# Modulation gates read back through DRAM, eight LayerNorm-1 tiles transposed by DMA in groups of four, loads in halves, and another order of tasks

## The chip, the cores and the metric

One NeuronCore of one Trainium2 chip runs the whole computation as one program. The metric is the time of the program on the device in microseconds (us). Before the change it is 209.67 us, the median of three runs (209.31 to 209.95).

A core has five instruction queues: TensorE (PE: matmuls, with PEld for the weight loads), VectorE (DVE), ScalarE (ACT), GpSimd (POOL) and SyncE (SP), which here issues nearly all DMAs. Each engine works off its queue in order and waits on semaphores of the others.

## The reference

One transformer block for 2048 tokens of width 512, with a linear attention of 32 heads and a gated feed-forward part of width 1376. A vector c gives six modulation vectors of 512: shift, scale and gate for each of the two parts.

```python
mod = (_silu(c) @ w_mod).reshape(c.shape[0], 6, 1, -1)
sa, ca, ga, sb, cb, gb = (mod[:, 0].copy(), mod[:, 1].copy(), mod[:, 2].copy(), mod[:, 3].copy(), mod[:, 4].copy(), mod[:, 5].copy())
h = _layernorm(x, axis=-1) * (1 + ca) + sa
x = x + ga * _A_ref(h, A_wqkv, A_w_phi, A_wo)
h = _layernorm(x, axis=-1) * (1 + cb) + sb
x = x + gb * _B_ref(h, B_w_gate, B_w_up, B_w_down)
```

In `_A_ref` q and k go through a small matrix per head, then through softmax(p) and softmax(-p) over the 16 features of a head; keys times values are summed over all tokens (kv), and each query's row is multiplied with that sum and divided by its normaliser. `_B_ref` is (sigmoid(h @ w_gate) * (h @ w_up)) @ w_down.

## The kernel before, in words

The 2048 tokens are 16 tiles of 128. All work is written as named tasks in a graph (`Graph`, line 103). A task has a name, one engine or a choice of engines, the keys that it reads and writes, and its buffers. The text `ORDER` (lines 35 to 81) lists every task once; `arrange` (line 131) walks it, takes the engine after an @ (A is ACT, D is DVE, P is POOL) or the first that the task allows, hands out buffers from fixed sets in the order in which they come free, and each engine gets its tasks in that order. The costs written beside the tasks do nothing when the kernel runs.

The names, in the order of the data:

- **ld_...** (lines 655 to 678): loads, issued by SP. x in pieces (x0a, x0b, x1, x2, x3), the thirds of wqkv (wk, wv, wq), w_mod (wm00 and wm01: shift and scale of the first part, one half of the rows each; wmga: its gate; wmm2: all three vectors of the second part), and wo, wg, wu, wd.
- **warm0, warm1_i** (line 711): matmuls on zeros ahead of the real work. **c1, c2, c3**: silu(c).
- **modc1, modc2** (line 717): shift and scale as columns, one column of 128 values per one-column matmul, 32 matmuls each; **modc1c, modc2c** copy them out of PSUM. **scb, ga, gb** (lines 693 and 898 to 906): silu(c) spread over 128 columns and multiplied with the gate's part of w_mod by four 512-column matmuls, so that the gate stands in every partition; **gac, gbc** copy it to SBUF. **wo0..3** and **wd0..10** multiply the rows of wo and wd with it (lines 908 and 917).
- **tpw, wTc, fold, foldc, wqT** (line 735): the small matrix w_phi is folded into the weights of q and k; wqT are DMA transposes.
- First LayerNorm (lines 775 to 840), in the groups of `LG`: **st1** statistics, **rs1** the inverse root, **nmr1** minus mean times it, **xn1** the normalised tile. Where `TD` is 0 the tile is transposed on TensorE (**tph**) and **hm1** applies scale and shift out of PSUM; where `TD` is 1 SP issues a DMA transpose per tile (**xT1**, line 816) and hm1 works in place in SBUF. hm1_20 is column block 0 of group 2.
- **K, V, Q**: the projections, 4 matmuls of 512 columns each. Keys: **e** both exponentials (ACT), **n** the sums over 16 features (DVE, line 869), **r** their inverse, **phi** the division (POOL, line 872), **va** the values' copy, **kv** the sum over tokens in PSUM. `NPART` cuts tile 11 in four parts and 13, 14 and 15 in two. e, phi, kvm, u and ga_sb share six buffers ("r2k").
- **perm, kvm, kvp, kvz, kvn** (lines 281 to 331): from the sum over tokens to the block-diagonal matrix for the queries. It needs all 16 tiles, so kvp0 parts the two halves of the kernel.
- Queries: **qe** exponentials, **sm, num, den, u** (tiles 0 to 7) or **num, z, dn, u** (tiles 8 to 15, lines 346 to 392), **o**, its transpose **oT**, **out** (times wo), **x1** (plus x).
- Second LayerNorm (**st2, rs2, nmr2, xn2, xnT, mod**), then in chunks of 1, 1, 2, 4, 4 and 4 tiles **g, u, tg, hm** (g3.10 is block 10 of chunk 3), **y** (down projection, one matmul per block), **fin** (plus x1) and **st** (store).
- **bnd..**, **ldf**: a check of the softmax's range, with a general path behind a branch that isn't taken here.

Around the change the order is set by three things: the text itself, the engines' in-order queues (SP's among them: a transpose that waits for its xn1 holds up every load behind it), and the semaphores. A gate that isn't there holds up wo, out, and TensorE with it.

Of the kernel before, what the change touches and what calls it, by code (L numbers as in the profile page):

```python
# [34 lines left out]
ORDER = """
wdz warm0 c1 warm1_0 warm1_1 warm1_2 pmem ld_x0b st1_3 st1_2 bd c2 rs1_2 warm1_3 ld_x0a st1_0 warm1_4 warm1_5 warm1_6 rs1_0 ld_wk ld_x1 st1_1 rs1_1 warm1_7
tpw3 tpw2 wTc2 tpw0 ld_wm00 ld_wm01 wTc0 tpw1 c3 wTc3@D nmr1_2 warm1_8 warm1_9 warm1_10 warm1_11 warm1_12 warm1_13 xn1_0 nmr1_1 wTc1 fold13 foldc13 xn1_2@P
fold11 fold10 tph03 tph01 fold12 foldc10 foldc11 foldc12 xn1_1@P xn1_3@P st1_5 ld_x2 st1_4 st1_6 st1_7 modc1.0 ld_wv tph02 tph23 tph21 rs1_3@P nmr1_3 modc1.1
modc1c tph20 tph13 warm1_14 tph00 hm1_20 hm1_01@A hm1_21@A hm1_03@A hm1_13 hm1_00 hm1_02 tph22 rs1_4@P nmr1_4 K0 tph10 hm1_22@A hm1_23@A K2 ld_wq st1_11 e0.0
xn1_4@P xn1_5@P xn1_6@P hm1_10@A st1_10 tph11 st1_9 st1_8 e2.0 hm1_11@A tph12 hm1_12@A V2 xn1_7@P tph31 K3 hm1_31 e3.0 tph43 tph30 K1 tph32 rs1_6@P nmr1_6  # L40
n0.0 hm1_43@A rs1_5@P nmr1_5 hm1_32 hm1_30 tph41 V0 tph33 e1.0 tph42 V1 tph40 n2.0 xn1_11@P xn1_10@P ld_x3 wqT3 ld_wo wqT0 r0.0@A hm1_33@A xn1_8@P xn1_9@P
hm1_41 va0 K5 hm1_42@A xT1_11 hm1_40@A va2 va1 tph52 K4 tph53 xT1_10 st1_13 r2.0 n1.0 phi0.0 e4.0 r1.0@A phi2.0 st1_12 tph51 tph50 V4 hm1_50@A hm1_53@A rs1_7
wqT2 phi1.0 n3.0 va4@D hm1_51 hm1_52 wqT1 nmr1_7 xn1_13@P xn1_12@P K6 n4.0 r3.0 r4.0 V3 V5 kv0.0 K7 kv1.0 kv2.0 hm1_62 hm1_61 va5 e5.0 e6.0 n5.0 va3@D e7.0
hm1_63 phi3.0 xT1_13 xT1_12 fold02 V8 r5.0 phi4.0 hm1_60 foldc02 va8 V7 V6 kv3.0 fold00 va7 st1_14 n7.0 r7.0 n6.0 K8 e8.0 phi5.0 hm1_72 K10 kv4.0 fold03 K11
warm1_15 hm1_70@P va6 r6.0@A e11.4 e11.6 hm1_71 kv5.0 phi7.0 hm1_73 n8.0 foldc00@D foldc03@D st1_15 r8.0 e11.0 phi6.0 V11 K9 e11.2 fold01 n11.6 ld_wd2 ld_wd
ld_wu perm e9.0 rs1_8 V10 K13 e13.4 n11.4 foldc01@D n11.2 n9.0 r11.6 nmr1_8 ld_wmga ld_wmm2 r9.0 kv6.0 kv7.0 phi8.0 va10 e10.0 e13.0 va11@D r11.2 V9 va9@D
r11.4 phi9.0 Q00 V12 Q03 xn1_14 xn1_15 qe00 kv8.0 Q10 phi11.2 phi11.4 kv9.0 qe03 n11.0 n10.0 tph81 tph83 phi11.6 r11.0 r10.0@A K12 hm1_81 hm1_83 tph80 tph82
Q13 hm1_82@A phi11.0 phi10.0 hm1_80 n13.0 K15 K14 r13.0 va12@D e12.0 kv10.0 e15.4 phi13.0 n13.4 r13.4@A phi13.4 e15.0 n12.0 r12.0 kv11.4 e14.0 e14.4 n15.4
n14.4 Q02 kv11.0 kv11.2 Q11 V13 ld_wg qe02 qe11 scb kv11.6 r14.4 n15.0 va13@D r15.4 n14.0 phi12.0 r14.0 r15.0 phi14.4 V14 V15 va15 va14 phi15.4 ga kv12.0
kv13.0 modc2.0 kv13.4 kv14.4 kv15.4 phi14.0 qe10 Q01 kvm1 gac kvp2 kvz2 kv14.0 phi15.0 kv15.0 qe01 Q32 kvm0 kvp1 kvp0 qe32 wo1@D wo2 kvz0 kvz1 gb kvn1@A kvn2  # L50
# [1066 lines left out]
```

## Time and profile before

| | |
|---|---|
| median of three runs | 209.67 us |
| the profiled execution | 209.63 us, its span 207.9 us |
| TensorE clock granted | 1.00 of full speed throughout |
| matmul and weight-load records | 1516 and 1539 |
| first 512-column matmul of the real work (K0) | starts at 13.34 us |
| second half of wm0 landed | 11.33 us |
| last phi of POOL ends, kvp0 starts | 56.3 us, 57.54 us |
| wmga and wmm2 issued | 36.24 and 36.79 us |
| DMA moved | 18.74 MB; 390 GB/s at most in a slice of 5.2 us |
| last fin ends | 205.26 us |

The profile's page gives the busy time of each engine, then the span in 40 slices, in which each digit is the busy share in tenths. Matmuls are pipelined and their ends are modelled, so TensorE's busy time says little of how close it is to its peak; the number of matmuls and the start of each say more. "SPq" stands for an issue of a DMA by SyncE, and "to landing" for the time from the issue to the semaphore. The chain of waits follows the work that ended last back from the end; the lines shown of it are start, length and what ran.

### The profile page before, as it was taken

To read this page: it belongs to the slowest core of one execution; us is meant where nothing else is said; L and a number is where in the kernel's file an instruction comes from. 1 tells how busy PE (TensorE), PEld (TensorE's weight loads), DVE (VectorE), ACT (ScalarE), POOL (GpSimd) and SP (SyncE) were. 2 spreads that over 40 slices of the span, in tenths; PEclk is the share of its full clock that TensorE was granted. 3 is DMA by queue.
4 is the path that set the end of the run, shared out by engine and by line. 5 is a ranking of instruction groups with operands and counts; after the bars stand their busy time and mean duration, and the time that the engine had idled before them with its cause. 6 is when DMAs were issued, how large, how long until landed. Compare 5 with 4: busy or idle time off the path is not lost.

```text
span 207.9 us, 4302 instructions
## 1 busy us (share of the span) xinstructions
PE 200.3 (96%) x1516; PEld 112.4 (54%) x1539; DVE 168.2 (81%) x459; ACT 107.9 (52%) x259; POOL 103.4 (50%) x137
## 2 busy tenths in 40 slices
PE   7789999999999999999999999999999999999994
PEld 2555465454675588976764544454444444444443
DVE  3999999999599998899988999979797815456642
ACT  2699999999886986524443322521244300142300
POOL 5589999999996989601337202633040612000000
PEclk9999999999999999999999999999999999999999
DMA  6995922999200201522032210342011131001011
GB/s 179 367 349 144 130 32 51 321 390 401 82 3 3 50 2 30 122 33 42 12 76 52 54 25 0 77 101 55 0 29 47 25 79 50 25 2 50 3 60 54
DMA packets 30893, 18.74 MB, mean 90 GB/s; under 512 B 20657, under 2 KB 28818, under 8 KB 30866
## 3 DMA queue, kind: packets, MB, share of 16 engines
q1 hardware_dynamic: 30336, 18.39, 31.6%
q8 instruction: 14, 0.23, 0.5%
q14 instruction: 13, 0.11, 0.2%
q10 hardware_dynamic: 530, 0.02, 0.1%
HBM read 11.58 MB, written 2.10 MB: 66 GB/s over the span
## 4 chain that ended last, share of the span: by engine, by line
PE 74%; ACT 7%; POOL 6%; DMA 4%; DVE 3%; issue 3%; SPq 1%; POOLq 0%; DVEq 0%
PE y_ps L606 18%; PE g_ps L568 17%; PE u_ps L568 17%; PE a_ps L477 6%; POOL phi L872 5%; PE q_ps L928 5%; DMA wmod_sb<-in_w_mod_dram 4%; ACT h1T L831 3%; ACT e L866 2%; DVE ks L869 2%; PE num L360 2%; PE num L444 2%; PE v_ps L854 1%; PE g_ps L570 1%; ACT tg L578 1%
## 5 line engine op out<-in xcount | busy, mean ns | idle before, releaser
L578 ACT ACTIVATE tg<-g_ps 128x512 bf16<-128x512 f32 (+4 forms) x66 | 28.7, 454 | 66.2 <-PE g_ps L568 50.5
L606 PE MATMUL y_ps<-wd_sb,wmod_sb 128*128 128x512 bf16 (+3 forms) x182 | 42.2, 366 | 0.2
L589 DVE SCALAR_TENSOR_TENSOR wmod_sb<-tg,u_ps 128x512 bf16<-128x512 bf16 (+4 forms) x63 | 30.0, 495 | 13.0 <-ACT tg L578 7.0
L872 POOL TENSOR_TENSOR phi<-e,ks 128x1024 bf16<-128x1024 bf16 (+2 forms) x22 | 31.5, 1453 | 0.5
L568 PEld LDWEIGHTS <-wu_sb 128*128 128x128 bf16 (+1 forms) x252 | 21.7, 99 | 15.4
L568 PEld LDWEIGHTS <-wg_sb 128*128 128x128 bf16 (+1 forms) x252 | 21.4, 99 | 15.2 <-issue 0.2
L606 PEld LDWEIGHTS <-wmod_sb 128*128 128x128 bf16 (+1 forms) x187 | 17.9, 98 | 16.5
L568 PE MATMUL g_ps<-wT_sb,wg_sb 128*128 128x512 bf16 (+2 forms) x121 | 23.8, 321 | 0.2
L568 PE MATMUL u_ps<-wT_sb,wu_sb 128*128 128x512 bf16 (+2 forms) x123 | 23.7, 322 | 0.1
L497 POOL TENSOR_SCALAR ve<-mv 128x2 f32<-128x2 f32 (+1 forms) x8 | 1.8, 223 | 41.2 <-DVE mv L487 41.2
L568 PE MATMUL g_ps<-wqk_sb,wg_sb 128*128 128x128 bf16 (+4 forms) x127 | 19.9, 287 | 0.1
L613 DVE TENSOR_TENSOR ot<-y_ps,x 128x512 bf16<-128x512 f32 (+1 forms) x17 | 11.1, 656 | 11.0 <-PE y_ps L606 10.5
L568 PE MATMUL u_ps<-wqk_sb,wu_sb 128*128 128x128 bf16 (+4 forms) x128 | 19.5, 287 | 0.0
L468 POOL TENSOR_TENSOR o<-u 128x512 bf16<-128x512 f32 x12 | 15.2, 1268 | 8.7 <-DVE u L435 4.7
L869 DVE TENSOR_REDUCE ks<-e 128x64 f32<-128x1024 bf16 (+2 forms) x22 | 19.4, 899 | 0.0
L866 ACT ACTIVATE e<-k_ps 128x512 bf16<-128x512 f32 (+2 forms) x44 | 18.1, 502 | 0.3 <-PE k_ps L850 0.2
L933 ACT ACTIVATE eT<-q_ps 128x512 bf16<-128x512 f32 x32 | 17.0, 622 | 1.3 <-PE q_ps L928 1.0
L850 PE MATMUL k_ps<-wqk_f,h1T 128*128 128x512 bf16 x62 | 15.8, 379 | 0.4 <-DVE h1T L833 0.3
L477 PE MATMUL a_ps<-wo_sb,oT 128*128 128x512 bf16 x61 | 15.8, 379 | 0.1
L928 PE MATMUL q_ps<-h1T,wqk_f 128*128 128x512 bf16 x58 | 15.6, 379 | 0.3
L854 PE MATMUL v_ps<-wv_sb,h1T 128*128 128x512 bf16 x62 | 15.6, 379 | 0.2
L782 DVE BATCH_NORM_STATS2 st<-x_sb 128x6 f32<-128x512 bf16 x16 | 10.7, 669 | 2.5 <-DMA x_sb<-in_A_x_dram 2.5
(158 smaller groups left out, 331.3 us busy)
## 6 DMA issues: line engine op xcount, KB each, us to landing
out_dram<-ot SPq DMA_DIRECT2D x15, 128.0 KB, 1.9
x_sb<-in_A_x_dram SPq DMA_DIRECT2D x3, 512.0 KB, 8.5
wmod_sb<-in_w_mod_dram SPq DMA_DIRECT2D x3, 512.0 KB, 7.5
wmod_sb<-in_w_mod_dram SPq DMA_DIRECT2D x1, 1536.0 KB, 14.9
...
```

What stands on the lines that cost most here:

```text
L477: pe.matmul(ap_[:], lhsT=oT[:, j, :], rhs=wo_sb[:, j, :], start=(j == 0), stop=(j == KT - 1))
L568: pe.matmul(ps[:fsz, 0:n], lhsT=w[:, j, ft * P:ft * P + fsz], rhs=h[:, j, 0:n], start=(j == 0), stop=(j == KT - 1))
L578: G.add(f"tg{k}.{ft}", {"ACT": 0.13 + n * 0.00083}, lambda e, tg=tg, g_ps=g_ps, fsz=fsz, n=n: act.activation(tg[:fsz, 0:n], g_ps[:fsz, 0:n ...
L589: dve.scalar_tensor_tensor(hm_all[:fsz, hm[k].slot, ft, 0:n], tg[:fsz, 0:n], 1.0, u_ps[:fsz, 0:n], op0=ALU.add, op1=ALU.mult)
L606: mm = pe.matmul(y[:, 0:c1 - c0], lhsT=hm_all[:fsz, hm[k].slot, ft, tl * P:(tl + 1) * P], rhs=wd_sb[:fsz, ft, c0:c1], start=(ft == 0), sto ...
L850: pe.matmul(kp[:], lhsT=h1T[:, j, t * P:(t + 1) * P], rhs=wqk_f[:, j, D:2 * D], start=(j == 0), stop=(j == KT - 1))
L854: pe.matmul(vp[:], lhsT=h1T[:, j, t * P:(t + 1) * P], rhs=wv_sb[:, j, :], start=(j == 0), stop=(j == KT - 1))
L866: act.activation(ee[:, ha:hb, s, :], kp[:, ha * DH:hb * DH].rearrange("p (h j) -> p h j", j=DH), ACT.Exp, scale=1.0 - 2.0 * s)
L869: dve.tensor_reduce(ks[:, ha:hb].rearrange("p h s -> p (h s)"), ee[:, ha:hb].rearrange("p h s j -> p (h s) j"), axis=AX.X, op=ALU.add)
L872: pool.tensor_tensor(ph[:, ha * 32:hb * 32].rearrange("p (h j) -> p h j", j=DH), ee[:, ha:hb].rearrange("p h s j -> p (h s) j"), ks[:, ha: ...
L928: pe.matmul(qp[:], lhsT=wqk_f[:, j, blk * P:(blk + 1) * P], rhs=h1T[:, j, cq * 512:(cq + 1) * 512], start=(j == 0), stop=(j == KT - 1))
L933: act.activation(eT[cq][:, s * 4 + blk, :], qp[:], ACT.Exp, scale=1.0 - 2.0 * s)
```

## The change

1. **Gates.** ga and gb aren't computed by 512-column matmuls any more. Each is computed as four columns by one-column matmuls, like shift and scale. The four columns of one gate are interleaved: column k holds the values p * 4 + k, so its weights are read with a step of four elements. The columns go to a small tile (gcol); SP writes them to a tensor in DRAM (gwa, gwb: 128 partitions, 16 bytes each), and reads that tensor back into all 128 partitions (gra, grb). The tasks scb, ga, gb, gac and gbc go. gra and grb stand in SP's queue among the loads.
2. **First LayerNorm.** Tiles 8 to 11 and 12 to 15 form two groups of four, transposed by DMA. Before, tiles 10 to 13 were, in two groups of two. Their hm1 may also run on DVE.
3. **Loads.** wk, wv, wq, wg and wu come in halves, x in pieces of two tiles. wk's halves are halves of its columns.
4. **phi** may also run on DVE; in the new order phi6, a quarter of phi11, and five halves of phi13, phi14 and phi15 do.
5. **Tiles 8 to 15 of the queries.** The z copies take 16 columns instead of 8, and dn works on whole rows of 32 out of SBUF: six instructions instead of ten, and it holds no PSUM bank.
6. **The end.** The last tile's y is cut at column 384 instead of 256. The permutation matrix has a tile of its own (bdp).
7. **`ORDER`** is another one throughout. It starts with K3, K2 and K0, not K0, K2 and K3.

```diff
-LG = [[0], [1], [2, 3], [4, 5], [6, 7], [8, 9], [10, 11], [12, 13], [14, 15]]
-TD = [0, 0, 0, 0, 0, 0, 1, 1, 0]
+LG = [[0], [1], [2, 3], [4, 5], [6, 7], [8, 9, 10, 11], [12, 13, 14, 15]]
+TD = [0, 0, 0, 0, 0, 1, 1]
...
+st1_5 tph22 tph21 tph20 foldc13 rs1_3 warm1_11 foldc12 xn1_0 st1_6 st1_7 ld_wm01 warm1_12 modc1.0 foldc10 modc1.1 xn1_1@P ld_x2a ld_x2b rs1_4@P warm1_13
+warm1_14 tph00 tph12 modc1c nmr1_3 xn1_5@P xn1_4@P tph13 warm1_15 tph23 hm1_21@A hm1_20 hm1_12 hm1_13 tph03 tph10 hm1_23 hm1_22@A hm1_10@A K3 nmr1_4 st1_10
...
+kv11.0 kv11.2 phi12.0 qe03 Q11 Q01 n14.4 n14.0 r14.4 r14.0 r15.0@A r15.4@A va12 va15 va14 qe01 Q13 kv12.0 kv13.4 phi14.4@D phi15.0@D phi14.0@D phi15.4@D
+ld_wmm2 gra ld_wg1 modc2.0 kv13.0 kv14.4 kv15.4 kv14.0 kvm1 kv15.0 Q32 kvm0 perm kvp2 kvp1 kvp0 wo2 wo0 wo1 wo3 wo_all modc2.1 wmod_free kvz2 kvz0 kvz1 qe11
+qe13 qe10 kvn2 sm0 sm2 modc2c Q23 sm1 gwb kvn0@A smS2 Q30 qe32 kvn1@A smS0@D den0 num00 den2 u00 num01 Q12 num31 num30 smS1 qe30 u01 num21 tpo0 den1 qe12 oT0
+u30 u31 Q31 num10 num20 num11 out0 u10 qe31 u11 qe23 Q21 qe21 x1_0 st2_0 o3 tpo1 sm4 u20 smS4@D Q33 Q20 rs2_0 oT1 nmr2_0 u21 xn2_0 qe20 den4 grb wd4 num71
...
-scb = cst.tile([P, KT, P], BF16, name="scb")
+bdp = cst.tile([P, KT, P], BF16, name="bdp")
+gcol = cst.tile([P, 8], FP32, name="gcol")
+gdr = [drp.tile([P, KT], FP32, name=f"gdr{i}") for i in range(2)]
...
-                        G.add(f"z{t}{i}", {"ACT": 0.24, "DVE": 0.13}, f_z, r=[("num", t, i)], w=[("z", t, i)], bufs=[ps, zS])
+                        G.add(f"z{t}{i}", {"ACT": 0.25, "DVE": 0.14}, f_z, r=[("num", t, i)], w=[("z", t, i)], bufs=[ps, zS])
+                    def f_small(e, zS=zS, m=m, den=den, cc=cc):
+                        es = [zS[:, 4 * s:4 * s + 4, 8:16] for s in range(2)]
                         for s in range(2):
-                            dve.tensor_tensor(mq[s], part(s, 0), zS[:, 1 - s], op=ALU.mult)
+                            dve.tensor_tensor(m[:, 0, 32 * s:32 * s + 32].rearrange("p (b n) -> p b n", n=8), zS[:, 4 * s:4 * s + 4, 0:8], es[1 - s], op=ALU.mult)
+                        dve.tensor_tensor(den[:, 0], m[:, 0, 0:32], m[:, 0, 32:64], op=ALU.add)
+                        dve.reciprocal(den[:, 0], den[:, 0])
...
-                steps[-2:] = [(CHUNKS[k] - 1, 0, 256), (CHUNKS[k] - 2, 0, 512), (CHUNKS[k] - 1, 256, 512)]
+                steps[-2:] = [(CHUNKS[k] - 1, 0, 384), (CHUNKS[k] - 2, 0, 512), (CHUNKS[k] - 1, 384, 512)]
...
-    load("wk", ["wk"], lambda e: sp.dma_start(wqk_sb[:, :, D:2 * D], wqkv_v[:, :, D:2 * D]), 512 * K1)
+    for h in range(2):
+        load(f"wk{h}", [("wk", h)], lambda e, h=h: sp.dma_start(wqk_sb[:, :, D + 256 * h:D + 256 * h + 256], wqkv_v[:, :, D + 256 * h:D + 256 * h + 256]), 256 * K1)
...
+                        w = wmod_sb[:, j, ch * P:(ch + 1) * P]
+                        if ch // KT in (2, 5):
+                            w = wmod_sb[:, j, (ch - ch % KT) * P:(ch - ch % KT + KT) * P].rearrange("p (m k) -> p k m", k=KT)[:, ch % KT, :]
...
+    modc_task("modca", list(range(8, 12)), ["wmod_ga", "wmod_ga"], ["gcola"], lambda ps: act.copy(gcol[:, 0:4], ps[:]), 0.2)
+    modc_task("modc2", list(range(12, 24)), ["wmod_m2", "wmod_m2"], ["mod2", "gcolb"], f_mc2, 0.5)
...
-        for j in range(KT):
-            pe.matmul(ps[:], lhsT=scb[:, j, :], rhs=wmod_sb[:, j, c0:c0 + D], start=(j == 0), stop=(j == KT - 1))
-    G.add("gb", {"PE": 0.87}, lambda e: f_mm(e, gb_ps, 5 * D), r=["scb", "wmod_m2"], w=["gb"], bufs=[gb_ps])
-    G.add("gbc", {"ACT": 0.6}, lambda e: act.mul(gb_bc[:], gb_ps[:], 0.5), r=["gb", "modc2ps"], w=["gbc"], bufs=[gb_ps])
-    G.add("ga", {"PE": 0.87}, lambda e: f_mm(e, ga_ps, 2 * D), r=["scb", "wmod_ga"], w=["ga"], bufs=[ga_ps])
+    def f_gw(i):
+        sp.dma_start(gdr[i][:], gcol[:, 4 * i:4 * i + 4])
+    def f_gr(i):
+        sp.dma_start(gb_bc[:] if i else ga_sb[:], gdr[i][:].rearrange("p k -> (p k)").unsqueeze(0).to_broadcast([P, D]))
...
-                G.add(f"hm1_{g}{j}", {e: w[e] for e in ("ACT", "POOL")}, f_m, r=[("h1raw", t) for t in ts] + ["mod1"],
+                G.add(f"hm1_{g}{j}", w, f_m, r=[("h1raw", t) for t in ts] + ["mod1"],
...
-            G.add(f"phi{t}.{a}", {"POOL": 0.08 + 1.77 * w}, f_p, r=[("kr", t, a)], w=[("phi", t, a)], bufs=[ee, ks, ph])
+            G.add(f"phi{t}.{a}", {"POOL": 0.08 + 1.77 * w, "DVE": 0.08 + 1.07 * w}, f_p, r=[("kr", t, a)], w=[("phi", t, a)], bufs=[ee, ks, ph], port=("POOL", "DVE"))
```

More of the change, by code (lines that the diff above doesn't have):

```diff
@@ L41 @@
[L41 to L44, printed above, removed]
@@ L692 @@
     G.add("c3", {"DVE": 0.5}, f_c3, r=["c2"], w=["scbf"], bufs=[c_ps])
-    G.add("scb", {"ACT": 0.62}, lambda e: act.activation(scb[:], sc_bf[:].unsqueeze(2).to_broadcast([P, KT, P]), ACT.Copy), r=["scbf"], w=["scb"])
     G.add("bd", {"POOL": 1.15}, lambda e: pool.tensor_tensor(
```

181 lines of the change are left out of this document (87 added, 94 removed).

## The prediction

> **What bounds it now.** I read the page first, then the stretches, the chain, and last single tiles. The profiled execution took 209.63 us: a span of 207.9 and 1.73 around it; the median of the runs shown is 209.67, so its own time stands for them.
>
> ```profile
> PE 200.3 (96%) x1516; PEld 112.4 (54%) x1539; DVE 168.2 (81%) x459; ACT 107.9 (52%) x259; POOL 103.4 (50%) x137
> ...
> PE   7789999999999999999999999999999999999994
> PEld 2555465454675588976764544454444444444443
> DVE  3999999999599998899988999979797815456642
> ACT  2699999999886986524443322521244300142300
> POOL 5589999999996989601337202633040612000000
> ```
>
> TensorE's row is full from the third slice on, but overlapping matmuls make that row look fuller than it is. So I counted: each of the 1539 weight-load records belongs to one matmul of the order text, in order, which gives every TensorE task its start. Against these starts I set the work, at 0.216 us for 512 columns (the four of gb below take 0.86). All matmuls together are 196.0 us. Ahead of K0, which starts at 13.34, stand 7.8 us (4.8 of it warm-up matmuls). From K0 to kvp0 (57.54) there are 42.8 us of work in 44.2; from kvp0 to the last y (204.3) 145.4 in 146.8; then 3.5 us of tail. **TensorE has 2.8 us of holes in 191**, so time is won by taking matmuls away, and lost wherever another engine cannot keep that pace.
>
> Before kvp0 all four engines are nearly full:
>
> ```profile
> 12.00:25.00 13.00, 12.40 (x79) 6.48 (x79) 12.66 (x33) 12.89 (x33) 12.61 (x16) 1.00 0.90 205
> 25.00:37.00 12.00, 11.85 (x107) 6.60 (x107) 11.93 (x21) 11.94 (x33) 11.84 (x10) 1.00 0.22 40
> 37.00:50.00 13.00, 12.89 (x103) 6.53 (x104) 12.49 (x29) 12.26 (x35) 12.70 (x15) 1.00 1.04 379
> ```
>
> In these rows of stretches the columns behind the length are busy time of PE, PEld, DVE, ACT and POOL: none has even 1 us in 13 to spare. From the chain I need the start and four prices:
>
> ```profile
> 3.41 7.92 DMA wmod_sb<-in_w_mod_dram
> 11.38 0.57 PE modc_ps L723 x16
> 12.24 2.17 ACT h1T L831 x5
> ...
> 57.92 0.86 PE gb_ps L901 x4
> 58.97 0.40 PE modc_ps L723 x16
> ...
> 62.61 0.45 PE num L444 x8
> ...
> 204.84 0.42 DVE ot L613
> ```
>
> The second half of the scale and shift columns lands at 11.33; behind it come modc1.1, the modulation and the first K.
>
> **TensorE's work.** Gates as columns remove ga and gb: 2 x 0.86 = 1.72. They add 32 one-column matmuls (16 in modca, 16 in modc2): sixteen take 0.40, so 0.80. Tiles 8, 9, 14 and 15 go to the DMA transpose: 16 transposes less at 0.45/8 = 0.056, so 0.90. Net -1.8. The after order also has 8.0 us of matmuls ahead of its first K (K3), 0.2 more, in a stretch where TensorE waits for data anyway. Behind the first K stand 2.0 us less: **-2.0**.
>
> **Strided weights.** The 32 gate columns load weights four elements apart; every weight load of before is packed, so no row has their price. Below: nothing, as packed (25 ns from one to the next in modc), and no reason for less. Above: the 96-column loads, which are not read in the four chunks that the other operands show, took 123 ns, so 32 x 0.098 = 3.1. The packed loads of the same matmuls are nearest; I take half again their spacing, **+0.4**. The Trainium skill (TensorE: Matmul & The Clock Gate, "Weight-path perf modes — Fast Weight Load (FWL) and DoubleRow") lists fast weight loading for packed and strided columns alike; by that the term is 0 and the time 207.7, and no run here shows it.
>
> **Start.** wk comes in halves of 256 columns, so in 1024 pieces of 512 B instead of 512 of 1 KB. DMA records show 50 ns for 1 KB and 20 ns for 256 B; 30 ns between them gives 1024 x 30/16 = 1.92 us against 1.60. As many bytes (2.5 MB) precede the end of wm01 as before, and eight issues at 0.5 reach it by 5.9 us, ahead of its data. So it lands 0.3 later. K3 needs its four 256-wide modulations (DVE 0.32 each, ACT 0.45, two 128-wide ones and nmr1_3 between them), about what K0 waited for: **+0.3**. If the ring of descriptors doesn't slow SyncE, below is 0; if SyncE's issues became the limit (0.95 to 1.15 us each for x2, wv and wq), above is +1.5.
>
> **The stretch up to kvp0.** Between first K and kvp2 I summed each engine's slots (start to start, back to back) over both orders: DVE 39.3 before, 40.5 after; ACT 41.1 and 40.2; POOL 41.2 and 31.8; PE 41.4 and 41.1. POOL gives up seven phi parts (one whole tile 1.89, five halves 1.01, a quarter 0.58: 7.5 us), fewer xn and rs. DVE takes those parts; the row nearest is DVE's one wo (two SBUF inputs, 512 elements, 0.92 below, of which I read 0.37 as waiting), so 0.6 per half and 1.1 per tile, 4.5 in all, partly paid by four vaug copies (0.55) and a wo that leave it. Bounds: ks on DVE reads the same 1024 elements in 1.20, and with waiting wo's 0.92 a half. Before, DVE waited 1.38 us for POOL's last phi ahead of kvm; that goes, since POOL is 9 us lighter. Next late is DVE itself, at the kvm masks. The 1.38 won pays the 1.2 that DVE carries more: **0**.
>
> **Transposes, loads.** Eight transposes at 1.2 us of SyncE each and 2.4 to 4.3 to landing replace four. xT1_13 and xT1_15 wait for xn1 on DVE (about 37 us), and wo, wd, wmm2, gra and wg1 queue behind them on SP. From 39 us 3.3 MB at the 0.38 MB/us of the third row land at 50; modc2.0 stands at about 53, so 2 to 3 us hide this; without them each us late is a us. hm1_60 and its three fellows have under 1 us before K13.
>
> **The gates' round trip.** gwa writes 128 pieces of 16 B long before gra reads. gra waits until kv12 frees its buffer, about 53.5, is 256 KB (x loads of that size: 3.0 to landing), lands at 56.5; four wo on POOL at 1.17 end at 61.2; out0 is due at 63. **0**, with 1.8 us of cover. The b side ends 3 to 4 us before y0 needs wd. Gone with the matmuls are ACT's scb (0.72), gbc and gac (0.6 each), off TensorE's path.
>
> **Behind kvp0.** z copies of 16 columns and smaller dn take about 5 us from DVE over eight tiles; DVE waits there (13.0 us ahead of L589), so 0. Half wg and wu loads: their g and u come 15 us later, 0. **Tail:** the last fin has 128 columns, not 256 (0.42): **-0.2**.
>
> Sum: -2.0 + 0.4 + 0.3 + 0 - 0.2 = -1.5: span 206.4, time **208.1**.
>
> **Rivals.** *DVE locked out by POOL (slower).* Both multiplied wo in the same microsecond:
>
> ```profile
> L908 POOL TENSOR_TENSOR wo_sb<-wo_sb,ga_sb x3: 1158/1172/1622, 56.3 to 59.0; 128x512 bf16<-128x512 bf16 x3
> ...
> L908 DVE TENSOR_TENSOR wo_sb<-wo_sb,ga_sb x1: 916/916/916, 57.1 to 57.1; 128x512 bf16<-128x512 bf16 x1
> ```
>
> DVE started at 57.08, POOL's first ended near 57.45 (0.37 later), and POOL's second took 0.45 more than 1.17: each stood still while the other ran. After, DVE has seven phi parts, hm1_51, 60, 61, 63, xn1_13 and 15 out of SBUF. The last four phi meet an idle POOL; nine can meet a phi of 1.93, on average half of it, 0.97. Five that do cost DVE 4.8; with some 1.4 us of room to TensorE, 3.4 arrive: 211.5. It is slower than before from about 2.9 us of such waiting on. For it: the rows. Against: a POOL with 9 us of gaps. The Trainium skill (SBUF — State Buffer, "Who interferes with whom") calls the shared port pair an exclusive lock, which speaks against this change; the 1622 ns agree.
>
> *Work gone, time not:* DVE's 40.5 in that stretch holds TensorE, whose 2.0 turn into holes: 209.6. For it: DVE's full rows; against: the 1.38 us wait that goes.
>
> *Gates late:* if gra stays behind the 1.5 MB load (14.9 us to landing before, against 3.0), wo ends 4.3 us later, out0 stands 2.5 longer: 210.6. Decides from a landing at 58.3 on.
>
> *Strided loads dear* (3.1): 210.8.
>
> **Chances.** Forecast and its better side (holes shrink by 1, strided free: 206.6) 0.60; work gone, time not 0.15; lock 0.14; gates late 0.07; strided 0.04. Range 206.6 to 211.2, which leaves half of the lock's cases out; the forecast alone has 206.6 to 209.0. Faster by over 0.3% (about what a measurement can tell from no change) 0.60, within it 0.15, slower 0.25.
>
> **What would show it.** First K at 13.6; kvp0 near 56.2; no wait of TensorE or DVE on gra; POOL not DVE's releaser; modc's weight loads 25 to 40 ns apart; last fin 0.2 to 0.3. Wrong would be: a DVE row with tensor ops stretched by 0.5 us and more, K13 or kvm late, out0 waiting for wo, modc2.0 for its load.

## The result, and the profile after

The changed kernel takes 212.66 us (median of four runs, 212.59 to 212.84) against 209.75 for the kernel before: a ratio of 1.0143, 95% interval 1.0125 to 1.0161. The profiled execution took 212.59, its span 210.9 against 207.9. The forecast, 208.1 with a range up to 211.2, was wrong in size and in sign. All times below are medians of undisturbed executions; one execution of e4 and the profiled one of e15 ran at granted clocks of 0.975 and 0.974 and are left out, and of e15's profile only lengths of VectorE's instructions are read.

The page after, its busy times and the slices of all five engines:

```profile
PE 201.6 (96%) x1547; PEld 111.6 (53%) x1547; DVE 168.4 (80%) x425; ACT 112.7 (53%) x272; POOL 92.6 (44%) x118
...
PE   7999999959999999989999999999999999999993
PEld 2654655425676589748764444445444444444442
DVE  3899999999979998998999899874857756563522
ACT  2899999679998996445253322442251551323200
POOL 3667997558947599944243312515030210000000
```

VectorE has 34 instructions fewer and gave up some 5 us of dn, yet is as busy as before (168.4 against 168.2). GpSimd gave up 11 us. TensorE's row has a dent in the ninth slice (42 to 47 us) that the row before did not have. The rows of stretches (length, then busy PE, PEld, DVE, ACT, POOL, then TensorE's clock, the DMAs' busy share and GB/s) show where:

```profile
12.00:25.00 13.00, 12.89 (x101) 7.02 (x100) 12.44 (x34) 12.56 (x32) 11.38 (x19) 1.00 0.94 223
25.00:37.00 12.00, 11.74 (x100) 6.16 (x98) 11.90 (x22) 11.60 (x29) 9.83 (x7) 1.00 0.86 226
37.00:50.00 13.00, 10.20 (x81) 5.06 (x80) 12.97 (x23) 10.11 (x29) 8.45 (x6) 1.00 0.75 237
```

From 37 to 50 VectorE alone is full, with 12.97 of 13, while TensorE falls from 12.89 to 10.20 and GpSimd from 12.70 to 8.45. An engine that is full while the others fall off is the first to look at. Its timeline there (start, length, instruction, xcount), then GpSimd's, then two rows of TensorE's:

```profile
35.59 0.40 DVE L814 TENSOR_SCALAR xn<-x_sb,mv,rs 128x512 bf16<-128x512 bf16 x1
35.91 1.22 DVE L877 TENSOR_TENSOR phi<-e,ks 128x1024 bf16<-128x1024 bf16 x1
37.05 2.12 DVE L814 TENSOR_SCALAR xn<-x_sb,mv,rs 128x512 bf16<-128x512 bf16 x1
39.09 1.21 DVE L874 TENSOR_REDUCE ks<-e 128x64 f32<-128x1024 bf16 x1
...
42.79 2.66 DVE L838 TENSOR_SCALAR h1T<-h1T,modc 128x512 bf16<-128x512 bf16 x3
```

```profile
37.09 1.93 POOL L877 TENSOR_TENSOR phi<-e,ks 128x1024 bf16<-128x1024 bf16 x1 [1.74 <-PE kvacc L278]
41.05 3.93 POOL L877 TENSOR_TENSOR phi<-e,ks 128x1024 bf16<-128x1024 bf16 x2 [2.03 <-DVE ks L887]
```

```profile
43.03 0.43 PE L278 MATMUL kvacc<-vaug,phi 128*128 128x68 bf16 x8 [1.29 <-POOL phi L877]
45.19 2.98 PE L855 MATMUL k_ps<-wqk_f,h1T 128*128 128x512 bf16 x13 [1.51 <-DVE h1T L838]
```

The same xn instruction takes 0.40 at 35.59, with GpSimd idle, and 2.12 at 37.05, where phi7 runs from 37.09 to 39.02. The last bracket closes the ring: GpSimd's next phi waits 2.03 for ks, which stands behind that xn on VectorE. Among all VectorE instructions I subtracted the usual time of their form: three stick out by over 0.5: this xn (xn1_15, +1.7), one of the three hm1 (hm1_61, 2.02 from 43.11, +1.6) and dn8's addition at 92.23 (1.22 instead of 0.19, +1.0). In the trace of before none does.

**Where the 3.0 us came from.** I use the prediction's count again, at its 0.216 us for 512 columns in both kernels, and call the start of a matmul less all work ahead of it its lag. Work ahead of the last matmul: 195.8 before, 194.1 after, -1.7. First K: lag 5.5 before, 4.8 after, -0.7. From there to kvp0 the lag grows by 1.45 before and by 4.87 after, +3.4. The two big holes there are 1.67 ahead of kv8.0 (43.03), which waits for phi8, and 1.51 inside K13 (45.19), whose second matmul waits for hm1_61; the first row puts 1.29 on the hole that the count gives as 1.67, because it goes by modelled ends. From kvp0 to the last y the lag grows by 1.7 before and 3.6 after, +1.9; the biggest hole is 1.44 ahead of g2.0 (94.91), which waits for VectorE's u behind dn8. Tail and rest 0.1. The sum is +3.0.

### The profile page after: what moved, and what is told of

Read it like the earlier page. It is cut to its first block, busy times and chain, and to the rows that moved or that the text cites. A ratio compares the mean times of both kernels' runs of the same rounds, so it can differ in the third digit from the quotient of the medians.

```text
span 210.9 us, 4333 instructions
## 1 busy us (share of the span) xinstructions
PE 201.6 (96%) x1547; PEld 111.6 (53%) x1547; DVE 168.4 (80%) x425; ACT 112.7 (53%) x272; POOL 92.6 (44%) x118
## 4 chain that ended last, share of the span: by engine, by line
PE 64%; DVE 16%; POOL 10%; DMA 4%; issue 3%; ACT 1%; SPq 0%; POOLq 0%; DVEq 0%; ACTq 0%
PE y_ps L600 15%; PE g_ps L562 14%; PE u_ps L562 14%; PE a_ps L471 4%; POOL phi L877 4%; PE q_ps L933 4%; PE k_ps L855 3%; DVE st L787 3%; PE v_ps L859 3%; POOL wd_sb L922 3%; DMA x_sb<-in_A_x_dram 2%; DVE h1T L838 2%; DMA wqk_sb<-xn 2%; DVE u L444 2%; PE kvacc L278 2%
## 5 line engine op out<-in xcount | busy, mean ns | idle before, releaser
L572 ACT ACTIVATE tg<-g_ps 128x512 bf16<-128x512 f32 (+3 forms) x66 | 28.9, 454 | 58.3 <-PE g_ps L562 39.2
L600 PE MATMUL y_ps<-wd_sb,wmod_sb 128*128 128x512 bf16 (+4 forms) x187 | 43.7, 367 | 0.0
L877 POOL TENSOR_TENSOR phi<-e,ks 128x1024 bf16<-128x1024 bf16 (+2 forms) x15 | 24.5, 1652 | 7.3 <-DVE ks L887 4.4
L462 POOL TENSOR_TENSOR o<-u 128x512 bf16<-128x512 f32 x14 | 17.7, 1271 | 21.0 <-DVE u L429 12.2
L562 PE MATMUL g_ps<-wqk_sb,wg_sb 128*128 128x256 bf16 (+4 forms) x128 | 19.8, 287 | 1.1 <-DVE u L429 1.1
L859 PE MATMUL v_ps<-wv_sb,h1T 128*128 128x512 bf16 x64 | 16.4, 379 | 0.1
L607 DVE TENSOR_TENSOR ot<-y_ps,x 128x512 bf16<-128x512 f32 (+2 forms) x17 | 11.0, 654 | 6.6 <-PE y_ps L600 6.5
L471 PE MATMUL a_ps<-wo_sb,oT 128*128 128x512 bf16 x64 | 16.3, 379 | 0.0
L515 ACT ACTIVATE xn<-x,nmr,rs 128x512 bf16<-128x512 f32 x14 | 11.1, 812 | 5.1 <-DVE nmr L498 5.1
```

Of the source, the lines that this page charges most:

```text
L462: G.add(f"o{t}", {"POOL": 1.3, "DVE": 0.62}, lambda e, ub=ub, o=o: engine(e).tensor_tensor(o[:], ub[0][:].rearrange("p h d -> p (h d)"), u ...
L471: pe.matmul(ap_[:], lhsT=oT[:, j, :], rhs=wo_sb[:, j, :], start=(j == 0), stop=(j == KT - 1))
L562: pe.matmul(ps[:fsz, 0:n], lhsT=w[:, j, ft * P:ft * P + fsz], rhs=h[:, j, 0:n], start=(j == 0), stop=(j == KT - 1))
L572: G.add(f"tg{k}.{ft}", {"ACT": 0.13 + n * 0.00083}, lambda e, tg=tg, g_ps=g_ps, fsz=fsz, n=n: act.activation(tg[:fsz, 0:n], g_ps[:fsz, 0:n ...
L600: mm = pe.matmul(y[:, 0:c1 - c0], lhsT=hm_all[:fsz, hm[k].slot, ft, tl * P:(tl + 1) * P], rhs=wd_sb[:fsz, ft, c0:c1], start=(ft == 0), sto ...
L859: pe.matmul(vp[:], lhsT=h1T[:, j, t * P:(t + 1) * P], rhs=wv_sb[:, j, :], start=(j == 0), stop=(j == KT - 1))
```

## The experiments

Ratios below are to runs of the kernel before on the same chip (medians 209.8 to 210.6), with their 95% intervals. Theory A: VectorE instructions stand behind GpSimd's. Theory B: the group of four is too coarse. Theory C: the gates' way through DRAM is dear.

| kernel | time, us | ratio | interval |
|---|---|---|---|
| e1 after, slow form of xn and hm1 | 216.56 | 1.0337 | 1.0269 to 1.0406 |
| e2 after, other form of dn's addition | 213.24 | 1.0181 | 1.0113 to 1.0248 |
| e3 after, two pairs for the last four | 215.17 | 1.0252 | 1.0207 to 1.0297 |
| e4 before + gates through DRAM, late | 214.38 | 1.0226 | 1.0168 to 1.0284 |
| e5 after, xn1_15 on GpSimd | 212.24 | 1.0120 | 1.0074 to 1.0165 |
| e6 e5 + three hm1 off VectorE | 211.38 | 1.0072 | 1.0038 to 1.0106 |
| e7 after, dn's addition as reduce | 213.32 | 1.0186 | 1.0133 to 1.0239 |
| e8 e6 and e7 together | 210.40 | 1.0007 | 0.9979 to 1.0034 |
| e9 after, phi7 to phi9 on VectorE | 213.33 | 1.0188 | 1.0136 to 1.0241 |
| e10 e8, gates by matmul again | 212.50 | 1.0114 | 1.0076 to 1.0152 |
| e11 e8, two wd behind unit 2 | 211.06 | 1.0055 | 1.0034 to 1.0076 |
| e12 e8, V7 ahead of kv2.0 | 209.84 | 0.9994 | 0.9973 to 1.0014 |
| e13 before + gates, early | 211.68 | 1.0081 | 1.0049 to 1.0113 |
| e14 before + half loads | 209.79 | 0.9983 | 0.9965 to 1.0001 |
| e15 before, three hm1 on VectorE | 214.01 | 1.0168 | 1.0142 to 1.0194 |
| e16 e13 + the change's dn | 211.44 | 1.0061 | 1.0038 to 1.0084 |
| e17 e12, less on VectorE | 210.42 | 0.9978 | 0.9947 to 1.0010 |
| e18 e17, gate a early | 209.59 | 0.9970 | 0.9950 to 0.9989 |

### The form of the instruction (e1, e2): a miss that corrected the theory

My first reading of theory A was that only the fast form, tensor_scalar, stands still.

```diff
-dve.tensor_scalar(xn[:], x_sb[:, t, :], mv1[:, t, 0:1], rs1[:, t:t + 1], op0=ALU.subtract, op1=ALU.mult)
+dve.scalar_tensor_tensor(xn[:], x_sb[:, t, :], mv1[:, t, 0:1], rs1[:, t:t + 1].to_broadcast([P, D]), op0=ALU.subtract, op1=ALU.mult)
 # likewise where a group moved by DMA is modulated on DVE
```

> The changed kernel with one thing altered: where VectorE normalizes a tile (xn1_13, xn1_15) or modulates a transposed tile group (hm1_51, hm1_60, hm1_61, hm1_63), the tensor_scalar with two scalars is written as a scalar_tensor_tensor whose second operand is the same scalar broadcast along the row. Same engine, same place in its queue, same values. Theory A (the 3 us lost ahead of kvp0 are VectorE instructions that stand still while GpSimd multiplies phi, and only instructions of this fast form do so): the xn at 37.05 falls from 2.12 us to 0.5 to 0.8, the three hm1 from 2.66 us to 1.5 to 2.0, the hole at kv8.0 (1.67 us) falls under 0.5, K13 starts 1.5 to 2.5 us earlier, kvp0 comes at about 57.3 instead of 59.15, and the time is about 210.9 (210.0 to 211.6). Theory B (the group of four tiles is too coarse: its last transpose comes late whatever the engine): K13 at 45 as before, time 212.7 within 0.4. Theory C (the gates' way through DRAM costs the time): 212.7 as well.

```diff
-dve.tensor_tensor(den[:, 0], m[:, 0, 0:32], m[:, 0, 32:64], op=ALU.add)
+dve.scalar_tensor_tensor(den[:, 0], m[:, 0, 0:32], 1.0, m[:, 0, 32:64], op0=ALU.mult, op1=ALU.add)
```

> The changed kernel with one instruction of dn altered: the addition of the two halves of the denominator, a tensor_tensor of 32 elements, written as scalar_tensor_tensor (times 1.0, plus). Theory A: nothing changes up to kvp0 (59.15); the addition of dn8, 1.23 us at 92.23 while GpSimd adds o, takes about 0.2 to 0.3, the hole ahead of g2.0 (1.44 us) falls to about 0.5, and the time falls by 0.5 to 1.0, to about 211.9. Theory B and theory C: no change, 212.7 within 0.3.

Both fell. The rows of the tiles (xcount: ns min/median/max) in e1, xn and hm1:

```profile
L814 DVE SCALAR_TENSOR_TENSOR xn<-x_sb,mv,rs x3: 722/734/2415, 9.7 to 37.6; 128x512 bf16<-128x512 bf16 x3
```

```profile
L838 DVE SCALAR_TENSOR_TENSOR h1T<-h1T,modc x4: 740/857/2416, 29.1 to 46.7; 128x512 bf16<-128x512 bf16 x4
```

The other form is slower by itself (0.73 instead of 0.40) and its longest stands as long on top (+1.7); likewise dn8's addition in e2, 1.225. So the form I chose was no way out: like dn's tensor_tensor, it reads two operands from SBUF. kvp0 came at 61.87 and the kernel was slower still. That the time followed VectorE's slots, 2.7 us at kvp0, fits theory A; of C it says nothing.

### Pairs instead of fours (e3)

```diff
-LG = [..., [8, 9, 10, 11], [12, 13, 14, 15]]
-TD = [0, 0, 0, 0, 0, 1, 1]
+LG = [..., [8, 9, 10, 11], [12, 13], [14, 15]]
+TD = [0, 0, 0, 0, 0, 1, 1, 1]
-... hm1_60 hm1_61 hm1_63 va9 hm1_62@A ... K13 ... K12 e12.0 n11.2 ... K15
+... hm1_60 hm1_61 hm1_63 va9 hm1_62@A ... K13 ... K12 hm1_72@A e12.0 hm1_70 hm1_71 hm1_73 n11.2 ... K15
```

> The changed kernel with its last four layer-1 tiles as two groups of two, both still by DMA transposes, modulated in 256 columns: 12 and 13 where the four were, 14 and 15 behind K12. K13 and K12 then need only the first pair, whose transposes are issued first. Theory B: K13 starts at 43.0 to 43.5 instead of 45.19, because it no longer waits for tiles 14 and 15, and the time falls by 1 to 1.5, to about 211.4. Theory A: xn1_15 still takes about 2 us, the hole at kv8.0 stays at 1.5 or more, the modulations still stand behind phi, K13 starts after 44.3 and the time is 212.1 to 213.0. Theory C: 212.7.

Theory B falls. K12 came at 45.25, with a hole of 1.38 inside K13, though K13 no longer needed tiles 14 and 15; and the second set of modulations brought a second stall and holes of 0.83 and 1.28 ahead of K15 and K14:

```profile
L838 DVE TENSOR_SCALAR h1T<-h1T,modc x7: 249/344/1952, 28.9 to 47.1; 128x256 bf16<-128x256 bf16 x6, 128x512 bf16<-128x512 bf16 x1
```

Two of these took 1.95 (at 42.80 and 47.06). A piece of half the columns stands as long as a whole one: the length goes with GpSimd's phi, not with the piece. The ratio is 1.1% above the changed kernel's; theory A had named 0.2% at most, and had not priced the second set.

### Off VectorE, one at a time (e5 to e8)

```diff
 # e5
-... K9 xn1_15@D e11.4 ...
+... K9 xn1_15@P e11.4 ...
 # e6: and
-... hm1_60 hm1_61 hm1_63 va9 ...
+... hm1_60@A hm1_61@P hm1_63@P va9 ...
 # e7 (and e8 = e6 + e7)
-dve.tensor_tensor(den[:, 0], m[:, 0, 0:32], m[:, 0, 32:64], op=ALU.add)
+dve.tensor_reduce(den[:, 0], m[:, 0].rearrange("p (s h) -> p h s", h=32), axis=AX.X, op=ALU.add)
```

> The changed kernel with one engine altered: xn1_15 on GpSimd instead of VectorE, at the same place of the order, where GpSimd stood idle for 1.74 us in the changed kernel's run. After the first four runs theory A reads: a VectorE instruction whose operands all lie in SBUF, row for row, and that meets the start of a long GpSimd instruction stands until that one's end, whatever its form (the scalar_tensor_tensor stood as long as the tensor_scalar). It expects xn1_15 to take 0.8 us on GpSimd at about 35.5, n9 on VectorE about 1.7 us earlier, the hole at kv8.0 (1.67 us) under 0.5, the stall of one hm1 piece to stay, kvp0 at about 57.5, and 211.0 (210.4 to 211.7). Rival (GpSimd is the bound of this stretch, and the stall only fills time in which phi is awaited): phi7 and phi8 move later by the 0.8 us put on GpSimd, the hole at kv8.0 stays over 1, and the time is 212.3 to 213.5.

> As the kernel with xn1_15 on GpSimd, and the three modulations of the last group taken from VectorE too: hm1_60 on ScalarE, hm1_61 and hm1_63 on GpSimd. Theory A: no VectorE instruction ahead of kvp0 is longer than its usual time by over 0.2 us; K13 no longer waits for a stalled piece, but for the slower engines (0.81 and 0.78 us each), so its hole is 0.3 to 1.0 instead of 1.51; kvp0 at about 56.8 and the time about 210.2 (209.5 to 211.0). Rival (GpSimd is the bound): phi9 and those behind it move later by 1.6 us and kvp0 is not earlier than with xn1_15 alone on GpSimd; 211 to 212.5.

> The changed kernel with dn's addition of the two halves put back to the instruction that the kernel before had, one tensor_reduce over the two halves; the products stay as the change made them. In the six traces so far no tensor_reduce on VectorE is lengthened beside GpSimd (some 150 overlaps), while the addition of dn8 took 1.23 us in each of four kernels, as tensor_tensor and as scalar_tensor_tensor. Theory A: dn8's addition takes 0.1 to 0.25, the hole ahead of g2.0 (1.44 us) falls to about 0.5, and the time falls by 0.6 to 1.0, to about 211.8. Rival (the hole at g2.0 comes from unit 2's modulation, late because four products into wd stand ahead of it on GpSimd, since gate b lands late): the hole stays at 1.2 or more and the time at 212.7 within 0.3.

> The changed kernel with all three: xn1_15 on GpSimd, hm1_60 on ScalarE, hm1_61 and hm1_63 on GpSimd, dn's addition as tensor_reduce. Theory A: the gains add, kvp0 at about 56.8, the hole at g2.0 at about 0.5, and the time is about 209.2 (208.4 to 210.2), level with the kernel before. If both rivals hold: 211 to 212.5.

In e5 the hole at kv8.0 (1.67) is gone, kvp0 comes at 57.52 as theory A said, and the hm1 stall stays (2.02). In e6 the hole inside K13 falls from 1.31 to 0.45. From first K to kvp0 the lag grows by 3.1 in e5 and 2.3 in e6, against 4.9 after. The times fall by less than expected (212.24 and 211.38): first K itself came at 13.0 and 13.6 in these profiles, 0.1 and 0.7 later than after, with the same code ahead of it. In e7 the reduce of dn8 takes its usual time and the hole ahead of g2.0 halves, from 1.44 to 0.76. The first two rows are from e7, the last is dn's addition in the changed kernel:

```profile
L385 DVE TENSOR_TENSOR cc<-smS,den x16: 179/188/583, 92.5 to 149.2; 128x32 f32<-128x32 f32 x16
L382 DVE TENSOR_REDUCE den<-m x8: 220/222/223, 91.9 to 148.4; 128x32 f32<-128x64 f32 x8
L382 DVE TENSOR_TENSOR den<-m x8: 191/192/1221, 92.2 to 149.2; 128x32 f32<-128x32 f32 x8
```

The next instruction with two operands in SBUF, a cc, now catches 0.39 of it (the 583). e7's median, 213.32, does not show the gain of its profile (span 210.4 against 210.9) and lies above the 211.8 expected; its interval is wide. e8 has all three, and is level with the kernel before: 1.0007, at 210.40 a little above the range expected for it. Its row of the same stretch shows VectorE no longer full and TensorE back:

```profile
37.00:50.00 13.00, 12.59 (x102) 6.42 (x99) 11.30 (x22) 12.87 (x38) 11.53 (x10) 1.00 0.90 285
```

So without the three stalls the 1.4% between the kernels are gone, with the same matmuls in the same order. Not all of that need be the stalls: in e5, e6 and e8 four instructions, some 1.6 us at their usual lengths, also left the full VectorE, and these runs don't part the two (e9 shows where two of the stalls come from, not what each is worth). Nor is e8 faster than before, though TensorE has 1.7 us less to do in it: its holes are 2.5 us more than before, 1.0 ahead of kvp0 and 1.5 behind it, and what makes these is open.

### Is GpSimd really the cause? (e9), and does it need the new order? (e15)

```diff
 # e9, from after
-... phi7.0 ... phi8.0 ... phi9.0 ...
+... phi7.0@D ... phi8.0@D ... phi9.0@D ...
```

> The changed kernel with phi7, phi8 and phi9 on VectorE instead of GpSimd, which then runs nothing beside xn1_15 and the three hm1 pieces; these stay on VectorE. Theory A (GpSimd's instruction is what they stand behind): xn1_15 takes 0.4 instead of 2.12 and each hm1 piece 0.4 (2.02 the longest before), while VectorE has 3 times 1.2 more to do: 3.6 more, 3.3 less, so kvp0 at 59 to 60 and 212.5 to 213.8. Rival (they stand for another reason, the transposes and loads that write SBUF at that time): at least one of them still takes over 1.5, VectorE is 3.6 later and the time is over 214.5.

The instructions stay where they were; only GpSimd is empty beside them. The same two tile rows, xn and hm1:

```profile
L814 DVE TENSOR_SCALAR xn<-x_sb,mv,rs x3: 382/402/407, 9.9 to 36.7; 128x512 bf16<-128x512 bf16 x3
```

```profile
L838 DVE TENSOR_SCALAR h1T<-h1T,modc x4: 402/403/595, 28.9 to 43.6; 128x512 bf16<-128x512 bf16 x4
```

2.12 has become 0.41 and 2.02 has become 0.40, with the transposes and loads still there and the work left on VectorE: GpSimd beside it is the cause of the two stalls. VectorE pays it back with the three phi (kvp0 at 59.05, time 213.33), as expected.

```diff
 # e15, from before
-G.add(f"hm1_{g}{j}", {e: w[e] for e in ("ACT", "POOL")}, f_m, ...)
+G.add(f"hm1_{g}{j}", w, f_m, ...)
-hm1_72 ... hm1_71 ... hm1_73
+hm1_72@D ... hm1_71@D ... hm1_73@D
```

> The kernel before with three of its modulations of the transposed pair 12, 13 (hm1_71, hm1_72, hm1_73, 128 by 256) on VectorE instead of ScalarE, at their places, where GpSimd multiplies phi. Theory A: at least one of them takes 1 to 2 us instead of some 0.25, as in the changed kernel, though the order is the old one; K13 or the phi behind it is late and the time is 0.5 to 2 more than the kernel before. Rival (the stalls need the new order, with its transposes and loads at that time): each takes 0.2 to 0.35, ScalarE is relieved by 1.4 us and the time is within 0.3 of the kernel before or a little less.

```profile
L833 DVE TENSOR_SCALAR h1T<-h1T,modc x3: 494/1962/1979, 35.8 to 38.1; 128x256 bf16<-128x256 bf16 x3
```

In the old order, two of three pieces that need about 0.34 take 1.96 and 1.98, and the kernel is 1.7% slower. That is 3.8 us, where theory A expected 0.5 to 2: the three pieces hold VectorE for 4.27 us, and nearly all of it reaches the end. The stall belongs to the pairing of the two engines, not to the new order.

### The gates (e4, e13, e10) and dn (e16)

e4 and e13 put the change's gates into the old order. e4 keeps the old places; e13 lets gate a's weights load early and puts ga_sb into the store of x1.

```diff
 # both, from before
-scb ... ga ... gac ... gb ... gbc
+modca.0 modca.1 modcac gwa ... gra ... modc2.0 modc2.1 modc2c gwb ... grb
 # e13
-ga_sb = Buf("r2k", [P, D], FP32, "ga_sb")
+ga_sb = Buf("x1", [P, D], FP32, "ga_sb")
-ld_wo ... K8 ... ld_wmga ... ld_wg
+ld_wmga ... K8 modca.0 modca.1 modcac gwa ... ld_wo ... ld_wg gra
```

> The kernel before, in its own order, with the gates' part of the change alone: both broadcasts by matmul out (8 matmuls of 512 columns), 32 one-column matmuls in, the two gates through DRAM; gate a's matmuls where scb was made, its load where the copy stood, gate b's matmuls moved up to modc2.0. The prediction's step: TensorE's work falls by 1.72 and rises by 32 times 27 ns, 0.86, and the round trip is covered, so 208.9 (208.5 to 209.4). Theory C: a write of about 4.5 us and a load of about 4.2 us put the products into wo behind 61 us instead of 56.3, out0 stands 1 to 3 us, and the time is 210.3 to 212. Theory A says nothing against the prediction's step here, as no normalization or modulation changes its engine: 208.9 if wo is in time.

> The kernel before, in its own order, with the gates' part of the change, and gate a's way made early: its weights' load changes places with wo's, its matmuls, its write and its load into ga_sb stand at K8 and behind wg's load (about 33 to 45 us), and ga_sb lies in the store of x1, which is free until 65 us; gate b's matmuls at modc2.0 as in the run with late gates. The prediction's step: TensorE's work falls by 1.72 and rises by 0.86, ScalarE loses 1.8 us of copies, the round trips are covered: 0.8 to 1.2 less than the kernel before, about 208.7 (208.2 to 209.4). Rival (wd's products come 4 us later on GpSimd, since gate b's way through DRAM stays late, and crowd o and rs2): within 0.3 of the kernel before, or slower by up to 1.

In e4 the "gates late" rival happens in full: the tile row of ga_sb names both engines that stood for it, and by how much.

```profile
  DMA ga_sb<-gdr: 7.0, 2
who waited for it (us, times):
  POOL wo_sb L917: 4.2, 1
  DVE wo_sb L917: 2.8, 1
```

At 214.38 it cost more than the 210.3 to 212 expected: the wo that waits 2.8 holds all of VectorE's queue behind it, and TensorE has holes of 3.08 ahead of sm1 and 0.95 ahead of modca.1.

In e13 nobody waits for ga_sb, wo starts at 56.14 as before (56.28), and still it is 0.8% slower. One part of the reason is in the stretch from kvp0 to out0, first before, then e13:

```profile
57.00:64.00 7.00, 6.89 (x109) 4.97 (x109) 6.66 (x21) 5.13 (x14) 6.54 (x6) 1.00 0.01 2
```

```profile
57.00:64.00 7.00, 6.38 (x92) 4.36 (x91) 6.62 (x22) 4.45 (x12) 6.29 (x6) 1.00 0.16 37
```

VectorE has 6.6 of 7 in both; TensorE lost gb's work and got holes for it (0.47 ahead of sm1, 0.52 ahead of Q31). There gb stood beside VectorE's chain, and taking it away won nothing. The rest, 1.4 ahead of u1.10 behind a transpose that took 4.3 us to land, is not settled: e16 does not have that hole and is as slow, though its first K also came 0.6 later (13.71 against 13.11).

```diff
 # e16: e13 and the change's z and dn, with the addition as tensor_reduce
```

> The kernel before with the gates' part made early, and the change's dn with the addition as tensor_reduce. The prediction called dn's saving (VectorE, 5 us over 8 tiles) off the path: within 0.3 of the kernel with the gates alone. If dn is on the path somewhere: 0.3 to 0.8 faster, about 208.1. If one of its products stands behind GpSimd (0.39 in the repaired kernel): up to 0.5 slower.

With 1.0061 against 1.0081 dn makes no difference that can be told, and a cc of dn took 1.04 instead of 0.19: the new dn brings stalls of its own into the old order too.

The other way round, e10 takes the gates out of the repaired new order.

```diff
 # e10, from e8
-modca.0 modca.1 modcac ... gwa ... gra ... gwb ... grb
+foldc02@D scb ... kv12.0 ga gac ... modc2c gb gbc wmod_free
-    scb = cst.tile([P, KT, P], BF16, name="scb")
+    scb = bd
```

> The kernel with all three repairs (xn1_15 on GpSimd, the three hm1 pieces off VectorE, dn's addition as tensor_reduce) and the gates' part of the change undone in its order: scb back (in the store of bd, behind the last fold), gate a's four 512-column matmuls and a copy on ScalarE ahead of kv13.4, gate b's behind modc2c, no DRAM. The prediction's step says that the gates' part is worth the work, 1.72 less 32 one-column matmuls of 27 ns, 0.86: this kernel is then 0.6 to 1.1 slower than the one with the repairs alone (210.4), 211.0 to 211.6. Rival (the way through DRAM gives it back, since wo and wd are multiplied 4 to 7 us later and crowd GpSimd): no slower than 210.4, within 0.3, or faster, with the holes behind out0 smaller by 0.8 or more in all.

Here the gates' part is worth 1.1% (1.0114 against 1.0007; 212.50 and 210.40 us), more than the 0.6 of work (1.72 less 32 one-column matmuls of 0.034) and than the 211.0 to 211.6 expected: TensorE's holes grow as well (0.62 ahead of kv15.4, 0.61 ahead of Q12, 0.5 more ahead of kv2.0), with ScalarE making scb and two copies. Theory C falls for the new order, where gate a's weights are there at 22 us.

### Loads (e14) and what is left (e11, e12, e17, e18)

```diff
 # e14, from before
-ld_wk ... ld_wv ... ld_wq ... ld_x1 ... ld_wg ... ld_wu
+ld_wk1 ld_wk0 ... ld_wv0 ld_wv1 ... ld_wq1 ld_wq0 ... ld_x1a ld_x1b ... ld_wg0 ld_wg1 ... ld_wu0 ld_wu1
```

> The kernel before with the half loads alone: each load of the change's list as two halves, one behind the other at the place of the whole. The prediction put them at nothing: within 0.5 of the kernel before, with K0 0 to 0.4 earlier, since the transposes of wk start on its first half. Rival (more packets and issues on one queue make later loads late): K0 or modc2.0 later by over 0.5 us and 0.5 to 1.5 slower.

0.9983, no difference that can be told; K0 at 13.46 against 13.34.

```diff
 # e11, from e8
-wd3 wd2 ... wd10 ... wd7 o6 ... rs2_2 ... xn2_2@P
+wd3 wd2 ... o6 ... rs2_2 ... xn2_2@P wd10 wd7
 # e12, from e8
-fold02 kv2.0 kv3.0 V7
+fold02 V7 kv2.0 kv3.0
```

> The kernel with all three repairs and two of the four wd products that stand ahead of o6, rs2_2 and xn2_2 on GpSimd (wd10, wd7) moved behind them. If what is left of the hole ahead of g2.0 (0.50) comes from unit 2's modulation behind these products: o6 2.3 us earlier, the hole gone, and 209.9 (209.4 to 210.3). If it comes from VectorE's queue: no change, 210.4 within 0.3, or the y0 and y1 matmuls wait for wd7 and wd10 and it is 210.7 to 211.5.

> The kernel with all three repairs and V7 moved ahead of kv2.0 on TensorE, so that the hole there (0.62, waiting for phi2 behind GpSimd's three xn) is filled by V7's 0.86. If the stretch up to kvp0 is TensorE's own now: 0.4 to 0.6 off, kvp0 at 56.5 and 209.9. If the phi chain on GpSimd bounds it: the hole returns at a later kv, kvp0 at 57.0 and 210.4 within 0.3.

e11 is a miss: the hole ahead of g2.0 grew from 0.50 to 1.21, but the run does not tell which queue had held it. Two VectorE instructions met GpSimd at new places in it, a modulation at 87.80 (0.79 instead of 0.36) and a cc at 90.96 (0.94 instead of 0.58), together about what the hole grew by. In e12 the hole of 0.62 is gone, but the growth from first K to kvp0 is 2.4 as in e8 (2.5): half of it came back at kv4.0 (0.35). The median is 0.6 lower, and the two intervals overlap.

```diff
 # e17, from e12
-mod01 ... mod21 ... z82@D
+mod01@A ... mod21@A ... z82
 # e18: and
-ld_wmm2 gra ld_wg1
+gra ld_wo ... ld_wmm2 ld_wg1     # ga_sb in the store of x1
```

> The kernel with the three repairs and V7 ahead of kv2.0, and three small VectorE instructions between out0 and g2.0 (the modulations mod01 and mod21, the copy z82) on ScalarE, which is idle for half of that stretch. If VectorE's queue bounds the stretch: the hole ahead of g2.0 falls by about 0.5, from 0.87, and the time is 0.3 to 0.6 under that kernel's 209.84, about 209.4, faster than the kernel before by up to 0.4 per cent. If GpSimd's late products bound it: the hole stays and the time is 209.8 within 0.3.

> The same, and gate a's load into ga_sb issued ahead of wo's load (at about 40 us instead of 56.6), with ga_sb in the store of x1. wo's products then start when GpSimd is free, at about 58 instead of 60.9, and every product behind them up to 3 us earlier. If GpSimd's late products bound the stretch ahead of g2.0: 0.3 to 0.8 under the run without this, about 208.9. If VectorE's queue does: no change, within 0.3 of it; or more VectorE instructions meet the start of a GpSimd product and it is up to 0.8 slower.

e17 is not told apart from e12. In e18 wo starts at 55.47 instead of 58.84 and the hole ahead of g2.0 is 0.53 instead of 0.77. It is the one version whose interval lies below the kernel before, 0.9970 (0.9950 to 0.9989); the changed kernel's lies above 1. That is weak: one of 18 versions, by 0.3%, and its profiled span is 207.9, that of the kernel before. Between e17 and e18 the runs do not decide.

## Why the prediction was wrong

- **TensorE's work, -2.0.** Right: the count of the records gives -1.8 in all.
- **Strided weights, +0.4.** Nearly right: 0.3. The loads by themselves, packed in the kernel before, then a stretch after with the strided ones of modca (xcount: ns min/median/max):

```profile
L723 PEld LDWEIGHTS <-wmod_sb x64: 95/96/98, 10.4 to 59.2; 128*128 128x128 bf16 x64
L723 PEld LDWEIGHTS <-wmod_sb x13: 117/118/118, 22.1 to 22.5; 128*128 128x128 bf16 x13
```

  From one to the next, strided loads start 33 to 37 ns apart, median 34, where packed ones start 25 apart; 32 x 9 ns is 0.3 us. The twelve-column halves of modc2 hide that, since only 8 of their 24 columns are strided:

```profile
56.66 0.65 PE modc_ps L723 x24
...
207.67 0.29 DVE ot L607
```

  The Trainium skill (TensorE: Matmul & The Clock Gate, "Weight-path perf modes — Fast Weight Load (FWL) and DoubleRow") lists fast loading for both patterns and gives no price for a strided load. The 0 that the prediction drew from it is not what this trace shows, though 9 ns are little beside the 98 extra of the 96-column loads.
- **Start, +0.3.** Its reason failed: the second half of wm0 landed at 11.27, against 11.33 before, and not 0.3 later. What the start is worth is not decided: first K came at 12.87, 0.5 earlier than before, but between 12.6 and 13.9 in the other kernels that share its code. Half loads alone do nothing (e14).
- **Up to kvp0, 0 (kvp0 forecast 56.2).** This is the step that failed: kvp0 came at 59.15. The prediction let a wait of 1.38 pay VectorE's extra 1.2 us, and took the slots of xn1_13, xn1_15, hm1_60, 61 and 63 at their usual 0.3 to 0.4. Two of these five, xn1_15 and hm1_61, took 2.12 and 2.02 beside a phi of GpSimd, 1.7 and 1.6 more than their slots, on an engine that has 12.97 busy of 13 us; e5, e6 and e9 show it, each in its own way. "POOL not DVE's releaser" was a bad test, too: nothing in the waits names GpSimd, since the time is inside the VectorE instruction. The other sign named, tensor ops stretched by 0.5 us and more, is the one that appeared.
- **Transposes and loads, hidden.** Right in the outcome, in part by luck: e3 shows that tiles 14 and 15 did not hold K13, and modc2.0 did not wait. But the sum given (39 us, and 3.3 MB at 0.38 MB/us) ends at 47.7 and not at 50, and wmm2 landed at 53.58. modc2.0 came at 56.47 only because TensorE was late; at the forecast's 53 it would have waited 0.6. "hm1_60 and its three fellows have under 1 us before K13" was right and should have carried a price: any stall there comes through whole.
- **Gates' round trip, 0.** No hole, in part by luck. gra was issued at 56.6 and not 53.5 and landed 4.2 later; wo ran from 60.9 to 65.5, out0 followed at 66.5 with no hole of its own. TensorE was late itself by then, so the delay was not seen; with out0 at the forecast's 63 it would have stood some 2.5. In e8 gra landed at 58.93, and out0 followed at 64.34 without a hole.
- **Behind kvp0, 0.** Wrong by 1.9. dn's saving was indeed off the path, but its new addition reads two operands from SBUF and stood 1.0 behind GpSimd's o at g2.0; e7's hole there is 0.7 shorter. The rest is spread over smaller holes (0.51 ahead of num131) and is not settled.
- **Tail, -0.2.** The last fin is 0.29 instead of 0.42, -0.13; the span's tail did not change (3.6 against 3.5).
- **The rivals.** "DVE locked out by POOL" is what happened, at 0.14 of the chances. It named the mechanism and rows for it and then discounted it for "a POOL with 9 us of gaps". The gaps did not help: phi7 came out of such a gap 0.04 us after xn1_15 began. It also looked no further than kvp0. The Trainium skill (SBUF — State Buffer, "Who interferes with whom") goes on to say that tensor_reduce never contends and that an instruction with two SBUF inputs does, against a GpSimd that reads SBUF; e1, e2 and e7 agree (2.416, 1.225 and 0.223 us).
- "Work gone, time not" fits gb in the old order (e13), where VectorE is busy 6.6 of 7 us, and is false of the gates in the new one (e10). Its 209.6 is 0.5 less than the 208.1 plus 2.0 that its words say, without a reason given.
